# Issuing a kernel's first block in the order of planned times, with one planned store for each unit's left-over rows

## The chip, the cores and the metric

The kernel runs on one core of a Trainium2 chip. The core has five engines with a queue each: PE (TensorE, matrix products), DVE (VectorE), ACT (ScalarE), POOL (GpSimd) and SP (SyncE, which here only issues DMA transfers). Each queue is worked off in order. The metric is the device time of one execution in microseconds (us); lower is better.

## The reference

Eight batches of eight heads with 576 rows of 64 numbers each go through a linear attention, and its output through a feed-forward layer, all in 32-bit floats:

```python
q_s = softmax(q, over the 64 numbers of a row)
k_s = softmax(k, over the 576 rows)
kv = einsum('bhsd,bhse->bhde', k_s, v)            # 64 x 64 per head
x = einsum('bhsd,bhde->bhse', q_s, kv)            # as 4608 tokens x 512
h = x @ w_in                                      # 512 x 2048
r = maximum(h, 0.0)
out = (s * (r * r) + b) @ w_out                   # 2048 x 512
```

## The kernel before

A **unit** u is two heads of one batch; a **pair** is two units, so a batch is two pairs. A **block** is the first 512 rows of one batch; the 64 rows of each batch that are left over (the "left-over x") are gathered in the DRAM tensor `xleft` and become a ninth block at the end. The feed-forward layer of a block runs in 16 **steps** t, one for each 128 columns of `w_in`: the four groups `h` of a step (12 products, line 1006, into PSUM tile `h`), then ACT and DVE make `r`, `gh`, `gl` out of `h`, then the four groups `o` (12 products with `w_out`, line 1069, into PSUM tile `acc`). In what follows "step 4's h" means these 12 products.

The first block is special, because everything is still arriving. `fetch(f)` loads the 512 KB of `w_in` and the 512 KB of `w_out` of step f into a tile `st`; `conv_w(f)` splits them into a high and a low part with three operations on ACT (lines 238, 245, 253) and three on DVE (lines 242, 248, 255). `q_stream(u)` makes the x of unit u: softmax of q, a turn on PE (`qT`), a copy to SBUF (`early`, line 468), the product with kv (`xp`, line 475), then ACT writes the high part of x (line 481) and the left-over rows into a corner of the tile `misc` (line 273, in `keep_left`), and DVE the low part (line 484). `k_stream` and `kv_stream` do the keys of pairs 0 and 1, `k_pair` and `kv_second` those of pairs 2 and 3. Pairs 0 and 1 are batch 0, whose x the first block needs; pairs 2 and 3 are batch 1, for the second block. Pairs 2 and 3 are loaded (`reload`) over the SBUF area of pair 0, so each waits until the pair before has been used.

The order of all queues comes from a planner, the class `Order`: each of these functions is a stream of operations `Op(engine, planned cost, due, needs, ...)`, and the planner picks the next one. For the first 451 operations it picks nothing: `FIRST` is a written list of stream numbers, and the next operation of that stream is issued, whatever the times. Each engine's queue then holds its operations in the order of that list. The instructions that an operation issues on other engines than its own are not known to the plan: `q_stream`'s ACT operation calls `keep_left`, which, once both units of a pair are there, issues the store of the left-over x on SP (line 280); `load_v`, an SP operation, issues three memsets on POOL for pair 2 (lines 310 to 312); `q_stream`'s exponential issues a memset on POOL (line 451), and `k_exp` another (line 520).

While PE waits early on, the planner fills in products whose result nobody reads (`unused`, line 1196), until the first `h` takes their PSUM tile.

Of the kernel before, what the change touches and what calls it, by code (L numbers as in the profile page):

```python
# [25 lines left out]
def attention_moe(ctx: ExitStack, tc: tile.TileContext, q, k, v, w_in, w_out, s, b, out):  # L26
    nc = tc.nc
# [3 lines left out]
    P = 128  # L31
# [11 lines left out]
    DUE_R = (-150.0, -149.0, -148.0, -140.0, -139.0, -138.0, -50.0, -49.0, -48.0, 0.0, 1.0, 2.0)  # L43
    DUE_SB, DUE_L = -60.0, {"sb": -150.0}
    FIRST = (
# [12 lines left out]
    )  # L58
    ON_ACT = (-1.0, -1.0, 1.0, -1.0, -1.0, 1.0, 1.0, 1.0, -1.0, 1.0, -1.0, 1.0, -1.0, -1.0, -1.0, 1.0)
    PACE = 6  # L60
    KN_ON = ('ACT', 'ACT', 'ACT', 'ACT')
    QF_ON = ('ACT', 'DVE', 'ACT', 'ACT', 'DVE', 'ACT', 'DVE', 'DVE')
    WARM = 0
# [45 lines left out]
    def v_tile(t):  # L109
        m = 4 * NQ * (D + 1)  # L110
        return t[:, 0:m].rearrange("p (h n e) -> p h n e", h=4, n=NQ), t[:, m:VW].rearrange("p (h e) -> p h e", h=4)
# [156 lines left out]
    def keep_left(u, x):  # L268
# [6 lines left out]
        if len(there) == 2 and pr < NP:  # L275
            store_left(pr)

    def store_left(pr):
        bb, hq = divmod(pr, NP // 2)
        nc.sync.dma_start(xleft[:, 2 * hq:2 * hq + 2, bb * LEFT:(bb + 1) * LEFT], xl_.pop(pr)[0])  # L280
# [25 lines left out]
    def load_v(pr):  # L306
        main, left = sources(pr)
        vt, rest = v_tile(tiles[pr][2])
        if pr == NP // 2:
            nc.gpsimd.memset(rest[LEFT:P, :, 0:D], 0.0)  # L310
            nc.gpsimd.memset(vt[:, :, :, D:D + 1], 1.0)
            nc.gpsimd.memset(rest[:, :, D:D + 1], 1.0)
        for h in range(4):
            nc.sync.dma_start(vt[:, h, :, 0:D], main(v, h, 1)[:, 0])
        nc.sync.dma_start(rest[0:LEFT, :, 0:D], left(v, 0, 4))
# [119 lines left out]
    def q_stream(u):  # L435
# [38 lines left out]
        for a, src in enumerate((slice(0, HB), slice(HB, S))):  # L474
# [3 lines left out]
            )  # L478
        yield Op("ACT", 0.62, due)
        xh, xl = [t[:, hp, :].rearrange("p (a c) -> p a c", a=2) for t in (xh, xl)]  # L480
        nc.scalar.copy(xh, xp[:, :, 0:HB])
        keep_left(u, xp[:, 1, HB:HB + LEFT])
        yield Op("DVE", 0.6, due, free=[tag], gives=[f"x{u}"])
# [668 lines left out]
    def reload(pr):  # L1152

        p = 0 if pr == NP // 2 else pr - 1

        def v_():
            yield Op("SP", 3.2, DUE_R[3 * pr + 2], needs=[f"kv{p}"], gives=[f"v{pr} there"], dma=(0.62,) * 4 + (0.3,))
            load_v(pr)

        return whole(pr, 0, "k", DUE_R[3 * pr], [f"kv{p}"]), whole(pr, 1, "q", DUE_R[3 * pr + 1], [f"qe{2 * p}", f"qe{2 * p + 1}"]), v_()  # L1160
# [43 lines left out]
    with tc.manual_schedule(engines={E.PE, E.DVE, E.Activation, E.Pool, E.SP}):  # L1204
# [6 lines left out]
            + [k_stream(u) for u in range(NP)] + [k_pair(pr) for pr in range(NP // 2, NP)]  # L1211
            + [q_stream(u) for u in range(2 * NP)]
            + [kv_stream(pr) for pr in range(NP // 2)] + [kv_second(pr) for pr in range(NP // 2, NP)]
# [37 lines left out]
```

## Time and profile before

| | |
|---|---|
| median of 3 runs | 882.7 us (882.3 to 883.28) |
| profiled execution | 881.91 us, span of the trace 880.1 us |
| PE busy | 851.9 us (97%) |
| DVE busy | 600.3 us (68%) |
| ACT busy | 435.5 us (49%) |
| DMA, share of 16 engines in the main queue | 31.4% |

Times in the trace are counted from the start of the span. A timeline row gives start, length, engine, line, operation, tiles, the number of instructions merged in it, and in brackets how long the engine sat idle before it and who ended that. "SPq" is the issue of a DMA, not the transfer.

### The profile page before, as it was taken

The page shows a single profiled execution, that of the slowest core. Times are in us where ns is not written, and L with a number is a line of the kernel's source. Part 1 is how long each engine was busy: PE and PEld are TensorE (multiplying, and loading weights), DVE is VectorE, ACT ScalarE, POOL GpSimd, SP SyncE. Part 2 cuts the span into 40 slices and gives each one's busy share as a digit, 9 for nine tenths or more (in the row PEclk, how much of TensorE's full clock was granted, in tenths as well). Part 3 has the DMA queues.
Part 4 walks back from the last instruction along what each step waited for, and adds up shares of the span by engine and source line. Part 5 has one row for each costly group of instructions (what it writes and reads, how often), then busy time and mean ns, then how long its engine had stood idle before and what let it go on. Part 6 is the DMA issues. An engine that isn't in the chain of part 4 may idle for free.

```text
span 880.1 us, 11806 instructions
## 1 busy us (share of the span) xinstructions
PE 851.9 (97%) x4385; PEld 702.1 (80%) x4385; DVE 600.3 (68%) x920; ACT 435.5 (49%) x736; POOL 167.3 (19%) x185
## 2 busy tenths in 40 slices
PE   7779989999999999999999999999999999999997
PEld 6567868888888888888888888888888878888886
DVE  5767867677879676869576956696677686765400
ACT  4767966453645444544444544363445465555300
POOL 1000000211112020202011201111023436872000
PEclk9979999999999999999999999999999999999999
DMA  8559043433444523352244314342430110000100
GB/s 255 161 181 346 8 147 85 132 82 92 102 137 91 131 73 112 73 127 61 75 90 127 75 46 129 89 105 63 129 88 1 51 48 1 1 1 0 49 25 24
DMA packets 106572, 79.45 MB, mean 90 GB/s; under 512 B 56212, under 2 KB 100244, under 8 KB 106388
## 3 DMA queue, kind: packets, MB, share of 16 engines
q1 hardware_dynamic: 105360, 77.60, 31.4%
q10 hardware_dynamic: 1156, 1.11, 0.4%
q8 instruction: 34, 0.56, 0.3%
q14 instruction: 22, 0.18, 0.1%
HBM read 60.29 MB, written 18.40 MB: 89 GB/s over the span
## 4 chain that ended last, share of the span: by engine, by line
PE 87%; DMA 4%; ACT 3%; DVE 2%; issue 1%; SPq 1%; POOL 0%; ACTq 0%; POOLq 0%; DVEq 0%
PE acc L1069 37%; PE h L1006 33%; PE q L896 6%; PE last L992 5%; DMA st<-in_moe_w_out_dram 3%; PE kv L328 2%; PE qa L896 1%; DMA st<-in_moe_w_in_dram 1%; PE xp L711 1%; PE xq L711 1%; PE xp L475 1%; ACT st L245 0%; ACT low L238 0%; PE kT L363 0%; ACT w L253 0%
## 5 line engine op out<-in xcount | busy, mean ns | idle before, releaser
L1006 PE MATMUL h<-x,w 128*128 128x512 f32 x1344 | 331.8, 394 | 6.2 <-ACT r L1031 5.6
L1069 PE MATMUL acc<-w,gh 128*128 128x512 f32 x1024 | 318.4, 392 | 0.0
L1006 PEld LDWEIGHTS h<-x,w 128*128 128x128 f32 x1344 | 253.1, 190 | 60.8 <-ACT r L1031 6.8
L1069 PEld LDWEIGHTS acc<-w,gh 128*128 128x128 f32 x1024 | 190.9, 188 | 39.3
L1069 PE MATMUL acc<-w,gl 128*128 128x512 f32 x512 | 199.7, 390 | 0.0
L1031 ACT ACTIVATE r<-h 128x512 f32<-128x512 f32 x112 | 66.9, 597 | 190.8 <-PE h L1006 186.6
L1044 DVE SCALAR_TENSOR_TENSOR r<-r,sb 128x512 f32<-128x512 f32 x105 | 82.5, 786 | 91.9 <-ACT r L1031 91.1
L1069 PEld LDWEIGHTS acc<-w,gl 128*128 128x128 f32 x512 | 96.2, 188 | 20.3
L1048 DVE SCALAR_TENSOR_TENSOR gl<-r,sb,gh 128x512 fp32r<-128x512 f32 x105 | 84.9, 808 | 32.4 <-ACT gh L1046 31.4
L1046 ACT ACTIVATE gh<-r,sb 128x512 fp32r<-128x512 f32 x105 | 76.0, 724 | 53.2 <-DVE r L1044 51.0
L610 POOL TENSOR_TENSOR area<-area,qm 128x640 f32<-128x640 f32 x24 | 32.7, 1374 | 153.0 <-DVE qm L608 147.1
L627 POOL TENSOR_TENSOR qe<-qe,qr 128x640 f32<-128x640 f32 x24 | 32.8, 1366 | 63.3 <-DVE qr L623 34.3
L992 PE MATMUL last<-w 128*128 128x512 f32 x192 | 43.7, 389 | 0.0
L992 PEld LDWEIGHTS last<-w 128*128 128x128 f32 x192 | 36.0, 188 | 7.5
L691 POOL TENSOR_TENSOR spare<-kvf,spare 128x256 fp32r<-128x256 f32 x12 | 10.3, 860 | 134.3 <-issue 125.6
L238 ACT ACTIVATE low<-st 128x1024 int32<-128x1024 uint32 (+1 forms) x17 | 18.4, 1091 | 22.4 <-DMA st<-in_moe_w_out_dram 21.2
L328 PEld LDWEIGHTS kv<-area 128*64 128x64 f32 x600 | 20.1, 143 | 9.7 <-issue 8.4
L966 DVE SCALAR_TENSOR_TENSOR gl<-r,sb,gh 128x512 fp32r<-128x512 f32 x16 | 16.2, 1015 | 16.7 <-ACT gh L964 16.7
L717 ACT COPY y<-xp 64x320 f32<-64x320 f32 x48 | 20.2, 421 | 14.8 <-PE xp L711 14.3
L597 ACT ACTIVATE area<-area 128x640 f32<-128x640 f32 x24 | 17.7, 737 | 18.5 <-DVE area L559 18.5
L328 PE MATMUL kv<-area 128*64 128x65 f32 (+1 forms) x600 | 22.4, 230 | 4.5 <-DMA area<-in_v_dram 3.0
L721 DVE TENSOR_TENSOR y<-xp,y 64x320 f32<-64x320 f32 x48 | 23.4, 488 | 1.1
(185 smaller groups left out, 1046.0 us busy)
## 6 DMA issues: line engine op xcount, KB each, us to landing
st<-in_moe_w_in_dram SPq DMA_DIRECT2D x16, 512.0 KB, 7.6
st<-in_moe_w_out_dram SPq DMA_DIRECT2D x16, 512.0 KB, 7.3
out_dram<-o SPq DMA_DIRECT2D x16, 512.0 KB, 2.6
turned<-area SPq DMA_DIRECT2D x24, 320.0 KB, 2.3
qT<-turned SPq DMA_DIRECT2D x48, 160.0 KB, 3.2
area<-in_k_dram SPq DMA_DIRECT2D x14, 512.0 KB, 4.4
area<-in_q_dram SPq DMA_DIRECT2D x14, 512.0 KB, 5.6
area<-in_v_dram SPq DMA_DIRECT2D x56, 128.0 KB, 4.9
```

Source lines behind the costliest of these rows:

```text
L328: nc.tensor.matmul(kv[h * D:(h + 1) * D, i], kt[:, i, h, n], vt(2 * i + h, n), start=(n == 0), stop=(n == NT - 1))
L610: nc.gpsimd.tensor_tensor(out=qt, in0=qt, in1=bc(qm, [P, 2, NT, D]), op=ALU.subtract)
L627: nc.gpsimd.tensor_tensor(out=qe_, in0=qe_, in1=qr, op=ALU.mult)
L721: nc.vector.tensor_tensor(out=y[half[h], at], in0=parts[h][a][half[h]], in1=y[half[h], at], op=ALU.add)
L896: nc.tensor.matmul(BANK[where], w(a)[:, c * P:(c + 1) * P], xs[b_][:, c], start=k in (0, 1, 3) and n == 0, stop=n == 5, skip_group_check=True)
L992: nc.tensor.matmul(t_, g[:, js], w_, start=(f == 0 and i == 0), stop=(f == NFC - 1 and i == 2))
L1006: nc.tensor.matmul(hp_, w[:, j, c, :], x[:, c, :], start=(c == 0 and i == 0), stop=(c == NP - 1 and i == 2))
L1031: nc.scalar.activation(r, hp_, AF.Relu)
L1044: nc.vector.scalar_tensor_tensor(out=r, in0=r, scalar=s_col, in1=r, op0=ALU.mult, op1=ALU.mult)
L1046: nc.scalar.activation(gh, r, AF.Identity, bias=b_col)
L1048: nc.vector.scalar_tensor_tensor(out=gl, in0=r, scalar=b_col, in1=gh.bitcast(F32), op0=ALU.add, op1=ALU.subtract)
L1069: nc.tensor.matmul(acc[blk, j // 2][:, j % 2], g[:, js], w_, start=(f == 0 and i == 0), stop=(f == NFC - 1 and i == 2))
```

## The change

`FIRST` is written anew. It now has 452 entries, and operations of different streams alternate in it in the order of their planned times, where before the operations of one stream often stood in runs. The store of the left-over x becomes a stream of its own, `left_out(u)`, one for each of the units 0 to 7, with an SP operation that the list places like any other; the memsets of pair 2's v become a POOL operation of the stream that loads it. Four entries of two small tables flip: `QF_ON` says on which engine `qT` of a unit is copied (units 5 and 6 trade places), `ON_ACT` whether a step's square is made on ACT or DVE (steps 6 and 11 go to DVE, step 12 to ACT).

```diff
+    DUE_O = (0.0,) * 8
     FIRST = (
-        0, 54, 54, 18, 0, 55, 55, 0, 2, 1, 48, 48, 54, 54, 54, 54, 31, 48, 55, 55, 31, 55, 48, 48, 1, 31, 1, 19, 49, 49, 49, 31, 31, 23, 56, 62, 56, 55, 54, 54,
...
+        0, 18, 0, 2, 19, 0, 1, 54, 23, 54, 48, 54, 55, 21, 55, 48, 20, 54, 48, 54, 55, 3, 48, 54, 31, 22, 49, 55, 48, 31, 1, 3, 55, 54, 31, 49, 4, 56, 49, 6,
...
-    ON_ACT = (-1.0, -1.0, 1.0, -1.0, -1.0, 1.0, 1.0, 1.0, -1.0, 1.0, -1.0, 1.0, -1.0, -1.0, -1.0, 1.0)
+    ON_ACT = (-1.0, -1.0, 1.0, -1.0, -1.0, 1.0, -1.0, 1.0, -1.0, 1.0, -1.0, -1.0, 1.0, -1.0, -1.0, 1.0)
-    QF_ON = ('ACT', 'DVE', 'ACT', 'ACT', 'DVE', 'ACT', 'DVE', 'DVE')
+    QF_ON = ('ACT', 'DVE', 'ACT', 'ACT', 'DVE', 'DVE', 'ACT', 'DVE')
...
+    def left_of(u):
+        return bits[:, u % 4 * LEFT:(u % 4 + 1) * LEFT]
+
+    def left_out(u):
+        bb, hp = divmod(u, NP)
+        yield Op("SP", 0.65, DUE_O[u], needs=[f"left{u} there"], gives=[f"out{u}"], dma=(0.1,))
+        nc.sync.dma_start(xleft[:, hp, bb * LEFT:(bb + 1) * LEFT], left_of(u))
...
     def load_v(pr):
-        if pr == NP // 2:
-            nc.gpsimd.memset(rest[LEFT:P, :, 0:D], 0.0)
-            nc.gpsimd.memset(vt[:, :, :, D:D + 1], 1.0)
-            nc.gpsimd.memset(rest[:, :, D:D + 1], 1.0)
...
-        yield Op("ACT", 0.62, due)
+        yield Op("ACT", 0.82, due, needs=[f"out{u - 4}"] if u >= 4 else (), gives=[f"left{u} there"])
-        keep_left(u, xp[:, 1, HB:HB + LEFT])
+        nc.scalar.copy(left_of(u), xp[:, 1, HB:HB + LEFT])
...
         def v_():
+            if pr == NP // 2:
+                yield Op("POOL", 1.0, DUE_R[3 * pr + 2], needs=[f"kv{p}"])
+                vt, rest = v_tile(tiles[pr][2])
+                nc.gpsimd.memset(rest[LEFT:P, :, 0:D], 0.0)
+                nc.gpsimd.memset(vt[:, :, :, D:D + 1], 1.0)
+                nc.gpsimd.memset(rest[:, :, D:D + 1], 1.0)
...
-            + [q_stream(u) for u in range(2 * NP)]
+            + [q_stream(u) for u in range(2 * NP)] + [left_out(u) for u in range(2 * NP)]
```

On PE the order of the first block stays nearly what it was, and the number of products that are not fillers stays exactly the same; the fillers go from 59 to 47. On ACT and DVE neighbours change places. The queues that change much are SP and POOL.

SP's queue while x of batch 0 is made, before. `st_438`, `st_370`, `st_116` and `st_539` hold the weights of steps 4, 2, 0 and 3; q and v are pair 2's; `xleft<-misc` is the store of the left-over x (units 0 and 1 the first time, 2 and 3 the second).

```order
L280 DMA xleft<-misc 128x2x64
L222 DMA st_438<-in_moe_w_in_dram 128x4x256
L224 DMA st_438<-in_moe_w_out_dram 128x1024
L224 DMA st_370<-in_moe_w_out_dram 128x1024
L303 DMA area<-in_q_dram 128x4x256
L304 DMA area<-in_q_dram 64x4x64
L224 DMA st_116<-in_moe_w_out_dram 128x1024
L280 DMA xleft<-misc 128x2x64
L222 DMA st_539<-in_moe_w_in_dram 128x4x256
L224 DMA st_539<-in_moe_w_out_dram 128x1024
L314 DMA area<-in_v_dram 128x4x64 x4
L315 DMA area<-in_v_dram 64x4x64
```

The same place after the change; `st_230`, `st_225`, `st_108` and `st_377` are the weights of steps 4, 2, 0 and 3, and k is pair 2's.

```order
L225 DMA st_230<-in_moe_w_out_dram 128x1024
L312 DMA area<-in_k_dram 128x4x256
L313 DMA area<-in_k_dram 64x4x64
L225 DMA st_225<-in_moe_w_out_dram 128x1024
L312 DMA area<-in_q_dram 128x4x256
L313 DMA area<-in_q_dram 64x4x64
L225 DMA st_108<-in_moe_w_out_dram 128x1024
L223 DMA st_377<-in_moe_w_in_dram 128x4x256
L225 DMA st_377<-in_moe_w_out_dram 128x1024
L319 DMA area<-in_v_dram 128x4x64 x4
L320 DMA area<-in_v_dram 64x4x64
L285 DMA xleft<-misc 128x64
```

No store stands between k and v of pair 2 any more; the first one, unit 0's alone, comes behind v. Step 4's weights have moved in front of k (their first half stands further up, in front of pair 1's v).

SP's queue around the last weights of the first block, before. `st_1082`, `st_1084` and `st_1091` are steps 13, 14 and 15; v is pair 3's; the store is that of units 4 and 5.

```order
L314 DMA area<-in_v_dram 128x4x64 x4
L315 DMA area<-in_v_dram 64x4x64
L280 DMA xleft<-misc 128x2x64
L222 DMA st_1082<-in_moe_w_in_dram 128x4x256
L222 DMA st_1084<-in_moe_w_in_dram 128x4x256
L224 DMA st_1084<-in_moe_w_out_dram 128x1024
L224 DMA st_1082<-in_moe_w_out_dram 128x1024
L222 DMA st_1091<-in_moe_w_in_dram 128x4x256
L224 DMA st_1091<-in_moe_w_out_dram 128x1024
```

And after the change, where `st_927`, `st_922` and `st_1046` are steps 13, 14 and 15 and the store is unit 4's alone.

```order
L223 DMA st_922<-in_moe_w_in_dram 128x4x256
L223 DMA st_927<-in_moe_w_in_dram 128x4x256
L285 DMA xleft<-misc 128x64
L225 DMA st_922<-in_moe_w_out_dram 128x1024
L225 DMA st_927<-in_moe_w_out_dram 128x1024
L319 DMA area<-in_v_dram 128x4x64 x4
L320 DMA area<-in_v_dram 64x4x64
L223 DMA st_1046<-in_moe_w_in_dram 128x4x256
L225 DMA st_1046<-in_moe_w_out_dram 128x1024
```

Two of the six weight transfers have moved in front of the store, and v behind it. The copy on ACT for which the store waits has moved too: before, it stood in front of step 10's `r`, now it stands behind step 8's.

POOL's queue, before: the memsets of units 2 and 3 (`qe_244`, `qe_361`), those behind pair 2's exponentials of k (line 520), those of pair 2's v (lines 310 to 312), and unit 5's (`qe_611`).

```order
L451 MEMSET qe_244 128x10
L451 MEMSET qe_361 128x10
L520 MEMSET area 64x2x64 x2
L310 MEMSET area 64x4x64
L311 MEMSET area 128x16
L312 MEMSET area 128x4
L451 MEMSET qe_611 128x10
```

After the change, with lines 456, 525 and 1165 to 1167 in these roles:

```order
L456 MEMSET qe_270 128x10
L1165 MEMSET area 64x4x64
L1166 MEMSET area 128x16
L1167 MEMSET area 128x4
L456 MEMSET qe_360 128x10
L525 MEMSET area 64x2x64 x2
L456 MEMSET qe_597 128x10
```

The memsets for v have moved from behind pair 2's exponentials to in front of unit 3's memset.

## Rows read from the trace of the kernel before

**Rows 1.** The page: PE's busy time, share and instructions, and the 40 slices of 22 us, PE's busy tenths and the granted clock in tenths.

```profile
PE 851.9 (97%) x4385; PEld 702.1 (80%) x4385; DVE 600.3 (68%) x920; ACT 435.5 (49%) x736; POOL 167.3 (19%) x185
PE   7779989999999999999999999999999999999997
PEclk9979999999999999999999999999999999999999
```

**Rows 2.** What PE waited for from 0 to 130 us: total, times, longest.

```profile
PE h L1006 <- ACT r L1031: 5.6, 3, 3.7
PE xp L475 <- ACT early L468: 4.2, 2, 3.9
PE kv L328 <- DMA area<-in_v_dram: 3.0, 2, 2.1
```

**Rows 3.** PE's timeline from 28 to 153 us, the rows at which the stretches of the argument begin.

```profile
28.87 1.39 PE L328 MATMUL kv<-raw 128*64 128x64 f32 x40
...
38.49 1.24 PE L475 MATMUL xp<-early,kvf 128*128 128x256 f32 x4 [3.86 <-ACT early L468]
...
45.50 3.52 PE L1006 MATMUL h<-x,w 128*128 128x512 f32 x12 [0.26 <-ACT r L1031]
...
56.56 0.30 PE L328 MATMUL kv<-area 128*64 128x65 f32 x2 [2.10 <-DMA area<-in_v_dram]
...
68.24 0.62 PE L1069 MATMUL acc<-w,gh 128*128 128x512 f32 x2
...
72.80 3.01 PE L1006 MATMUL h<-x,w 128*128 128x512 f32 x12 [1.67 <-ACT r L1031]
...
79.24 2.88 PE L1006 MATMUL h<-x,w 128*128 128x512 f32 x12
81.96 0.62 PE L1069 MATMUL acc<-w,gh 128*128 128x512 f32 x2
...
124.29 4.60 PE L1006 MATMUL h<-x,w 128*128 128x512 f32 x12 [3.67 <-ACT r L1031]
...
132.03 2.88 PE L1006 MATMUL h<-x,w 128*128 128x512 f32 x12
...
152.48 2.88 PE L1006 MATMUL h<-x,w 128*128 128x512 f32 x12
```

**Rows 4.** What SP's queue waited for from 0 to 130 us: total, times, longest.

```profile
SPq L280 <- ACT misc L273: 39.5, 3, 24.4
...
SPq L314 <- POOL qe L451: 10.9, 1, 10.9
```

**Rows 5.** SP's timeline, the issues on either side of its long waits (a start and the time of issuing).

```profile
21.69 0.61 SPq L304 DMA_DIRECT2D area<-in_k_dram  x1
29.60 0.37 SPq L280 DMA_DIRECT2D xleft<-misc  x1
30.02 0.46 SPq L222 DMA_DIRECT2D st<-in_moe_w_in_dram  x1
...
42.47 0.50 SPq L224 DMA_DIRECT2D st<-in_moe_w_out_dram  x1
53.82 2.61 SPq L314 DMA_DIRECT2D area<-in_v_dram  x4
...
85.55 2.48 SPq L315 DMA_DIRECT2D area<-in_v_dram  x1
112.49 0.39 SPq L280 DMA_DIRECT2D xleft<-misc  x1
```

**Rows 6.** The chain that ended last, in order of time: its transfers of weights in this stretch (start, us from issue to landing).

```profile
32.90 7.23 DMA st<-in_moe_w_out_dram
...
60.14 9.87 DMA st<-in_moe_w_out_dram
...
114.31 6.21 DMA st<-in_moe_w_out_dram
```

**Rows 7.** ACT's timeline from the copy of unit 2's `qT` to step 0's `r`, the rows before which it sat idle, and the first.

```profile
31.46 0.64 ACT L468 COPY early<-qT 128x576 f32<-128x576 f32 x1
35.55 2.37 ACT L238 ACTIVATE low<-st 128x1024 int32<-128x1024 uint32 x2 [3.44 <-DMA st<-in_moe_w_out_dram]
...
40.21 0.71 ACT L238 ACTIVATE low<-st 128x512 int32<-128x512 uint32 x1 [1.17 <-DMA st<-in_moe_w_out_dram]
...
41.75 1.71 ACT L245 ACTIVATE st<-st 128x512 f32<-128x512 f32 x2 [0.24 <-DVE st L242]
44.85 0.60 ACT L1031 ACTIVATE r<-h 128x512 f32<-128x512 f32 x1 [1.39 <-PE h L1006]
```

**Rows 8.** DVE's timeline: step 2's `gl`.

```profile
59.28 0.68 DVE L1041 TENSOR_TENSOR gl<-r,gh 128x512 fp32r<-128x512 f32 x1
```

**Rows 9.** Stretches of 10 us: busy time (and instructions) of PE, PE's weight loads, DVE, ACT, POOL; granted clock; DMA share; GB/s.

```profile
20.00:30.00 10.00, 9.38 (x136) 7.72 (x134) 9.85 (x18) 8.81 (x21) 0.28 (x1) 1.00 0.43 122
...
60.00:70.00 10.00, 9.65 (x56) 8.14 (x57) 0.00 (x0) 0.00 (x0) 0.00 (x0) 0.82 1.04 370
70.00:80.00 10.00, 8.21 (x38) 6.26 (x38) 7.98 (x13) 9.87 (x15) 0.23 (x1) 1.00 1.08 350
80.00:90.00 10.00, 10.00 (x46) 8.17 (x45) 9.86 (x15) 9.15 (x14) 0.00 (x0) 1.00 1.00 277
90.00:100.00 10.00, 10.00 (x49) 8.22 (x49) 8.64 (x11) 9.83 (x13) 0.12 (x1) 1.00 0.00 0
```

22 rows, old and new, of the table FIRST are left out of this document.

## The prediction

> **What bounds the kernel now.** I read the page first: PE is busy for 97% of the span, and the slices in which it is not, and in which its clock is not full, are nearly all in the first six, 130 us [rows 1]. So the question is only what PE loses there, since the change leaves PE's products the same but for fillers. The list of PE's waits names three kinds: products `h` waiting for `r`, `xp` for the copy `early`, `kv` for the transfer of v [rows 2]. PE's timeline gives the places: a gap of 3.86 us before 38.49, then slow products; 2.10 us at 56.56 and more around it; 1.67 us at 72.80; 3.67 us at 124.29, after which 12 products take 4.60 us instead of 2.88 [rows 3]. From 132.03 to 152.48 and on there is no gap.
>
> None of these has its cause on PE, ACT or DVE. ACT and DVE did nothing at all from 60 to 70 us, while the DMA engines ran at 370 GB/s [rows 9]: the work waited for weights. And the weights were late because SP's queue stood still, as SP's own waits show: 39.5 us in three waits for the copy on ACT (line 273) whose result the store of the left-over x carries, and 10.9 us for POOL, which had to do pair 2's memsets first [rows 4]. SP's timeline gives the places: nothing issued from 22.30 (21.69 + 0.61) to 29.60, from 42.97 to 53.82, and from 88.03 to 112.49 [rows 5]. The chain shows what came of it: the last transfer of step 0's `w_out` was issued at 32.90 and landed at 40.13, another landed at 70.01, another at 120.52 [rows 6], and each landing is where ACT wakes.
>
> **The change, step by step.** The stores leave the places where they blocked, and the memsets for v come as soon as pair 0's kv is done. I follow the new order with the old durations, in four stretches, each from one row to the next.
>
> *To step 0's `r` (44.85 before).* On ACT, from the end of unit 2's copy, 32.10 (31.46 + 0.64), to `r` at 44.85 are 12.75 us, of which it sat idle 3.44 + 1.17 + 0.24 + 1.39 = 6.24 [rows 7]; 6.5 us is work, and the change keeps these operations. Ahead of it, pair 1's kv (28.87) now stands behind one of step 0's groups, a quarter of 2.72 us (81.96 − 79.24) [rows 3], so the start moves to 32.8. Without the waits `r` comes at 39.3, **5.6 us** earlier. Are the weights there? Before, from the restart at 30.02 to the landing at 40.13 took 10.1 us, with step 4's weights first [rows 5, 6]. Now SP goes on at 22.3, and step 4's weights are already in the queue: the landing is at about 32.4, and 2.8 us later (1.05 MB at 370 GB/s [rows 9]) if those still have to be worked off. ACT wants them about 3.4 us after 32.8, at 36.2. The wait on DMA goes either way.
>
> *To step 1's last group and step 2's first `o` (68.24 before, 23.4 us after `r`).* On ACT and DVE, from that `r` to the end of step 2's `gl` (59.28 + 0.68 = 59.96) took 15.1 us [rows 7, 8] without a long DMA wait; that stays. PE has in this time three times h, one `kv` of 1.39, two times four groups of o or h, in all 5 × 2.72 + 1.39 + 0.3 = 15.3. The two hand results to each other, so I take 15.7. What falls away is the wait for pair 2's v, issued at 53.82 before [rows 5]; now it follows step 3's weights and lands before 40, and PE wants it at about 48. Step 2's o starts at 39.3 + 15.7 = 55.0, and this stretch gives 23.4 − 15.7 = **7.7 us**.
>
> *To step 14's `h` (132.03 before, 63.8 us later).* PE has nine h and ten o, 19 × 2.72 = 51.7, and three turns of q, two `xp` and two turns of maxima, which take 0.2 to 1.0 each in the same timeline, 4.1 in all: 55.8. Before, the stretch held the waits of 1.67 and 3.67 and the slow products behind the latter. The weights of steps 5 to 8 now follow v at about 1.4 us each and land from about 39 to 48, wanted from 54 on. The long block of 24.4 us is replaced by a store whose copy on ACT stands behind step 8's `r`, about 85.5 by this count, with only two weights of steps 13 and 14 behind it; by the 6.21 us of the last chain transfer [rows 6] they land by 94, wanted at about 97, behind step 10's `r`. So no wait: **8.0 us**. ACT and DVE must keep up: from 70 to 100 us they were busy 9.6 and 8.8 of 10 on average while PE had no gap behind 72.80 [rows 3, 9]. They can, barely.
>
> *To the second block's first `h` (152.48 before).* PE's work is the same. But unit 6's `xp` now comes only three products (0.68 us) behind pair 3's kv, with about 0.3 us on DVE and 1.0 on ACT between them; before, twelve products stood there. I take a loss of **0.9 us**; none if ACT is early, 2 if it is busy.
>
> Nothing else counts. Eight stores instead of four cost SP 4 × 0.4 us [rows 5] that hides behind the transfers. The memsets now stand ahead of unit 3's on POOL and wait for pair 0's kv; unit 3's memset waited for unit 1's turn on PE anyway, which PE does behind pair 0's kv in both orders. The flipped table entries move some 1.4 us from ACT to DVE over three steps, hidden where PE leads. Beyond 152 us PE was without gaps, so the whole gain is kept.
>
> The sum: 5.6 + 7.7 + 8.0 − 0.9 = 20.4 us. The profiled execution took 881.9, 0.8 less than the median of 882.7; I take the sum off the median and forecast **862.4 us**.
>
> The best possible: from 28.87 to 132.03 are 103.2 us, and PE's full-rate work in it is 25 × 2.72 + 10.4 of small products = 78.4, so 24.7 us can go, 858. The forecast leaves 3.4 us of gaps in it.
>
> *A page weighed against a row.* The fillers end earlier, at step 0's first group, and gaps of up to about 1 us stay between short products from 30 to 40 us. From 20 to 30 us the clock was at its full 2.4 GHz with 136 short products, most of them turns, and 9.38 us busy [rows 9]; behind the gaps of 3.67 and 3.86 us it was not. The Trainium skill, "TensorE: Matmul & The Clock Gate", part 4, says transposes don't count as busy for the clock; by that the stretch after 30 us would be slow, and the sum 865.4 (priced below) instead of 862.4. The rows of 20 to 30 us speak against it. What it would do is a rival below.
>
> **Rivals.**
> - *ACT and DVE become the bound.* Before, they had paused 10 us ahead of the full stretch; now they run through from 30 us. ACT's 9.87 of 10 from 70 to 80 [rows 9] speaks for it, PE's gapless run beside it against. If each of ten steps loses 0.5 us: 867.4.
> - *The transfers are the bound.* Moving step 4's weights ahead delays k and q of pair 2. If the landing that I put at 32.4 takes twice its 10.1 us, `r` is back where it was at 5.6 us more: 868. Against it: the DMA share was 0.43 from 20 to 30 us [rows 9], so there is room.
> - *The clock stays low from 30 to 45 us.* Step 1's h would take 3.52 [rows 3] to twice 2.72: about 3 us, 865.4.
> - *The change does not do what it says*: SP is stuck elsewhere, for instance at the load of pair 3's q, which waits for unit 4's exponential and has all weights from step 9 on behind it, and gives half of the gain back: 872.
> - *Slower.* Pair 3's v has moved behind that store and lands at about 95 instead of 88. The second block hangs on it through kv and unit 6. It decides only from a landing after 118, where kv stands, and makes the kernel slower than before only after 139: 885. No row shows a transfer 40 us late except behind a blocked SP.
>
> **How the numbers follow.** Forecast 0.62 (859 to 866), ACT and DVE 0.13, transfers 0.10, clock 0.06, half given back 0.05, slower 0.04. The range of 858.5 to 870 leaves out the last two and the tail. A measurement of this kernel can tell about 0.2% from no change, 1.8 us. Faster by more: 0.94; within: 0.02; slower: 0.04.
>
> **What would show it.** Right: in SP's timeline no gap over 5 us before 40 us, and stores that wait for nothing that another transfer needs; ACT's idle time for weights under 3 us where it was about 20; step 0's `r` near 39, step 2's o near 55, step 14's h near 111, the second block's first h near 132; PE's granted clock full from 30 us on. A first `r` after 42, or ACT or DVE named as releaser of PE in many small waits, would prove the sum wrong in its first or third term; a long wait at unit 6's `xp` the fourth. What would upset it altogether is a new wait of SP on an engine, in front of weights.

## The result

| | before | changed |
|---|---|---|
| median, run together | 882.5 us (880.07 to 883.28, 4 runs) | 860.33 us (860.12 to 860.66, 4 runs) |
| profiled execution, its span | 881.91, 880.1 | 860.22, 858.4 |
| ratio | | 0.9754, 95% interval 0.9734 to 0.9773 |

The change makes the kernel 2.5% faster. The forecast was 862.4 us, with a range of 858.5 to 870.

The page of the changed kernel answers [rows 1]: PE's busy time, its 40 slices (here of 21.5 us), and the granted clock.

```profile
PE 843.3 (98%) x4373; PEld 695.9 (81%) x4373; DVE 601.3 (70%) x921; ACT 434.5 (51%) x734; POOL 171.1 (20%) x185
PE   7899999999999999999999999999999999999997
PEclk9999999999999999999999999999999999999999
```

PE is busy for 8.6 us less although its products are the same but for twelve fillers of about 0.1 us each: the slow ones are gone. ACT and DVE are as busy as they were. Of the first six slices, 7, 7, 7, 9, 9, 8 before, two below 9 are left, and no slice has a low clock.

What PE waited for from 0 to 130 us answers [rows 2] (total, times, longest; left out are two waits ahead of 13 us).

```profile
PE xp L480 <- ACT early L473: 1.4, 2, 1.1
PE h L1011 <- DVE x L489: 1.0, 1, 1.0
PE xp L480 <- ACT kvf L350: 0.5, 1, 0.5
PE kn L381 <- ACT qe L457: 0.5, 1, 0.5
PE h L1011 <- ACT r L1036: 0.5, 1, 0.5
```

No transfer stands in this list any more, and the waits for `r`, 5.6 us before, are 0.5. PE's timeline has the marks of the four stretches, as in [rows 3] (lines are 5 higher in the changed file):

```profile
38.55 3.02 PE L1011 MATMUL h<-x,w 128*128 128x512 f32 x12 [0.47 <-ACT r L1036]
...
53.84 0.62 PE L1074 MATMUL acc<-w,gh 128*128 128x512 f32 x2
...
109.78 2.88 PE L1011 MATMUL h<-x,w 128*128 128x512 f32 x12
...
117.35 1.39 PE L333 MATMUL kv<-area 128*64 128x65 f32 x40
118.66 0.97 PE L1011 MATMUL h<-x,w 128*128 128x512 f32 x3
120.12 1.24 PE L480 MATMUL xp<-early,kvf 128*128 128x256 f32 x4 [0.49 <-ACT kvf L350]
...
130.97 2.88 PE L1011 MATMUL h<-x,w 128*128 128x512 f32 x12
```

From 38.55, where the wait of 0.47 ends, to 119 us no row has a bracket: PE never waits. SP's timeline answers [rows 5], its waits from 0 to 130 us [rows 4]:

```profile
20.62 1.50 SPq L313 DMA_DIRECT2D area<-in_k_dram  x1
22.17 0.60 SPq L225 DMA_DIRECT2D st<-in_moe_w_out_dram  x1
...
25.70 0.34 SPq L225 DMA_DIRECT2D st<-in_moe_w_out_dram  x1
...
29.32 5.56 SPq L319 DMA_DIRECT2D area<-in_v_dram  x4
...
37.10 0.55 SPq L285 DMA_DIRECT2D xleft<-misc  x1
...
63.56 7.44 SPq L223 DMA_DIRECT2D st<-in_moe_w_in_dram  x2
86.15 0.34 SPq L285 DMA_DIRECT2D xleft<-misc  x1
86.54 0.90 SPq L225 DMA_DIRECT2D st<-in_moe_w_out_dram  x2
```

```profile
SPq L312 <- PE kv L333: 32.0, 3, 24.6
SPq L285 <- ACT misc L487: 15.1, 1, 15.1
```

SP still waits for a store, 15.1 us from 71.0 (63.56 + 7.44) to 86.15, and this costs nothing, since only the `w_out` of steps 13 and 14, pair 3's v and the last weight stand behind it. What changed is not that SP waits less, but what stands behind it when it does. Pair 2's v is issued at 29.32 instead of 53.82.

Stretches of 10 us, which answer [rows 9] (busy time of PE, its weight loads, DVE, ACT, POOL; granted clock; DMA share; GB/s):

```profile
20.00:30.00 10.00, 9.20 (x105) 7.31 (x101) 9.88 (x19) 9.53 (x24) 0.83 (x4) 1.00 1.08 323
30.00:40.00 10.00, 7.51 (x32) 5.15 (x33) 9.05 (x15) 8.27 (x15) 0.00 (x0) 1.00 1.01 253
40.00:50.00 10.00, 10.00 (x79) 8.14 (x79) 9.92 (x13) 9.97 (x14) 0.59 (x4) 1.00 1.05 363
50.00:60.00 10.00, 10.00 (x48) 8.31 (x47) 9.21 (x15) 8.07 (x10) 0.12 (x1) 1.00 0.83 270
60.00:70.00 10.00, 10.00 (x47) 8.18 (x46) 8.59 (x13) 9.61 (x15) 0.00 (x0) 1.00 0.99 318
70.00:80.00 10.00, 10.00 (x48) 8.29 (x47) 9.54 (x14) 9.02 (x13) 0.00 (x0) 1.00 0.37 113
```

Before, the transfers ran at 122 GB/s from 20 to 30 us and at 350 to 370 from 60 to 80; now they run at 253 to 363 GB/s all the way from 20 to 70. DVE and ACT, idle from 60 to 70 us before, are full from 40 to 50 us, and PE beside them has no gap.

### The profile page after: what moved, and what is told of

Its sections match the earlier page's. It is cut to its first block, busy times and chain, and to the rows that moved or that the text cites. A ratio compares the mean times of both kernels' runs of the same rounds, so it can differ in the third digit from the quotient of the medians.

```text
span 858.4 us, 11791 instructions
## 1 busy us (share of the span) xinstructions
PE 843.3 (98%) x4373; PEld 695.9 (81%) x4373; DVE 601.3 (70%) x921; ACT 434.5 (51%) x734; POOL 171.1 (20%) x185
## 3 DMA queue, kind: packets, MB, share of 16 engines
q10 hardware_dynamic: 1156, 1.11, 0.4%
## 4 chain that ended last, share of the span: by engine, by line
PE 93%; DMA 3%; DVE 1%; ACT 1%; issue 1%; SPq 1%; ACTq 0%; DVEq 0%
PE acc L1074 40%; PE h L1011 36%; PE q L901 7%; PE last L997 5%; PE kv L333 2%; DMA area<-in_q_dram 2%; DMA st<-in_moe_w_in_dram 1%; PE qa L901 1%; PE xp L716 1%; PE xq L716 1%; PE xp L480 0%; DVE w L971 0%; SPq L313 0%; PE qT L470 0%; DVE misc L960 0%
## 5 line engine op out<-in xcount | busy, mean ns | idle before, releaser
L1074 PEld LDWEIGHTS acc<-w,gl 128*128 128x128 f32 x512 | 96.2, 188 | 20.2
L604 POOL MEMSET area<- 64x128 f32 x24 | 4.8, 200 | 102.4 <-issue 74.8
L722 ACT COPY y<-xp 64x320 f32<-64x320 f32 x48 | 20.2, 420 | 9.6 <-PE xp L716 8.9
L734 DVE TENSOR_TENSOR x<-y,x 128x512 fp32r<-128x512 f32 x24 | 23.4, 975 | 0.0
L1100 ACT COPY last<-last 128x512 f32<-128x512 f32 x3 | 1.8, 587 | 42.7 <-PE last L997 42.7
```

The source lines that it names most:

```text
L734: nc.vector.tensor_tensor(out=xl, in0=x, in1=xh.bitcast(F32), op=ALU.subtract)
L1074: nc.tensor.matmul(acc[blk, j // 2][:, j % 2], g[:, js], w_, start=(f == 0 and i == 0), stop=(f == NFC - 1 and i == 2))
```

## The experiments

For each kernel, the table gives the median and range of its runs, and from its profile step 0's `r` and the three stretches behind it: to step 2's first `o`, on to step 14's first `h`, on to the second block's first `h`. From there to the end of the span it was 727.2 to 727.7 us in every profile, so the four columns hold all of the difference but for some tenths.

| kernel | us | `r` | to `o` of 2 | to `h` of 14 | to `h` of 16 | span |
|---|---|---|---|---|---|---|
| before | 882.5 | 44.85 | 23.39 | 63.79 | 20.45 | 880.1 |
| changed | 860.33 | 37.90 | 15.94 | 55.94 | 21.19 | 858.4 |
| before again | 879.05 | 44.15 | 23.43 | 61.58 | 20.45 | 877.3 |
| stores alone | 869.27 (868.62 to 870.93) | 38.23 | 23.39 | 57.68 | 20.45 | 867.4 |
| memset alone | 872.51 (871.49 to 873.01) | 44.84 | 15.94 | 62.20 | 20.45 | 871.1 |
| stores and memset | 860.97 (860.13 to 862.13) | 38.75 | 15.95 | 56.01 | 20.45 | 858.8 |
| order alone | 860.23 (859.48 to 860.81) | 38.67 | 15.95 | 55.94 | 21.20 | 859.0 |
| stores early | 862.25 (860.31 to 863.19) | 39.85 | 16.97 | 55.94 | 21.20 | 861.4 |
| tables old | 860.32 (860.12 to 861.58) | 37.72 | 15.94 | 56.14 | 21.48 | 858.7 |
| memset in v | 859.76 (859.29 to 860.73) | 37.89 | 15.94 | 55.94 | 21.20 | 858.3 |
| less ahead | 860.47 (859.73 to 861.18) | 36.98 | 16.17 | 55.94 | 21.20 | 857.9 |
| xp later | 861.88 (861.41 to 862.56) | 37.70 | 15.93 | 55.94 | 23.12 | 860.1 |
| changed again | 860.63 (860.18 to 862.28) | 40.01 | 15.93 | 55.94 | 21.20 | 860.5 |
| kv behind h | 861.07 (860.79 to 863.21) | 38.12 | 15.93 | 55.94 | 21.92 | 859.3 |

Times are counted from each span's start; beside them the kernel before ran at medians of 880.9 to 882.1 us, 878.1 to 885.3 in single runs.

**Stores alone.** Each unit's store becomes a stream of its own in the kernel before; all else stays.

```diff
-        keep_left(u, xp[:, 1, HB:HB + LEFT])
+        nc.scalar.copy(left_of(u), xp[:, 1, HB:HB + LEFT])
...
-        9, 9, 7, 7, 37, 39, 37, 59,
+        9, 9, 7, 7, 383, 384, 385, 386, 37, 39, 37, 59,
...
-        61, 45, 45, 17, 47, 47, 60, 80,
+        61, 45, 45, 17, 387, 388, 47, 47, 60, 80,
```

> The kernel before, with each unit's store as an operation of its own (those of units 0 to 3 issued behind weight 5's w_out, those of 4 and 5 behind weight 15's); the order of all other operations, the memset and the tables stay. Theory of the prediction: SP is no longer held from 22.30 to 29.60 nor from 33.5 to 41.54, so step 0's r comes at 39 to 40 instead of 44.85 (5 to 6 us), pair 2's v still waits for the memset until about 48, and some of the third stretch goes too (W13 and W14 land earlier): 868 to 873 us. Rival (the gain comes from the new order of the operations on PE, ACT and DVE): 880 to 883 us, and r within 1 us of 44.85.

Measured 869.27 us, ratio 0.9866 (0.9846 to 0.9887): as the theory says, in its places too. `r` comes at 38.23, the second stretch keeps its 23.39, the third gives 6.1 of the 63.79. The first row is SP's timeline, the second PE's, the third SP's list of waits:

```profile
47.35 2.60 SPq L322 DMA_DIRECT2D area<-in_v_dram  x4
```

```profile
50.24 0.30 PE L336 MATMUL kv<-area 128*64 128x65 f32 x2 [2.89 <-ACT w L253]
```

```profile
SPq L322 <- POOL qe L459: 19.6, 1, 19.6
```

What SP was held by before is gone, and it runs into the next wait the sooner: pair 2's v now waits 19.6 us for POOL instead of 10.9.

**Memset alone.** In the kernel before, the memset becomes an operation of POOL's own, placed behind pair 0's kv.

```diff
+                yield Op("POOL", 1.0, DUE_R[3 * pr + 2], needs=[f"kv{p}"])
...
-        50, 50, 20, 62, 62, 50, 50, 56,
+        50, 50, 20, 62, 27, 62, 50, 50, 56,
```

> The kernel before, with only the memset as an operation of POOL's own right behind pair 0's kv; stores, order and tables stay. Theory of the prediction: step 0's r stays at 44.8 (within 0.5 us), since the stores hold SP as before; pair 2's v is issued at about 43 instead of 53.82, and the stretch from r to step 2's first o shrinks from 23.4 to 15 to 17 us; the third stretch loses little: 871 to 876 us. Rival 1 (v2 was not what PE waited for in this stretch): 881 to 883 us. Rival 2 (the loads behind v2, now 10 us earlier, free the third stretch as well): 865 to 869 us.

Measured 872.51 us, ratio 0.9899 (0.9880 to 0.9918). `r` stays at 44.84, and the second stretch is 15.94 us, the changed kernel's to the hundredth. SP's timeline, then PE's:

```profile
43.91 2.79 SPq L310 DMA_DIRECT2D area<-in_v_dram  x4
```

```profile
115.23 4.61 PE L1002 MATMUL h<-x,w 128*128 128x512 f32 x12 [3.45 <-ACT r L1027]
```

The store of units 4 and 5 still holds what stands behind it, and PE's wait for it and the slow products behind it are still there: the third stretch gives only 1.6 us, less than the 2.2 by which the two profiles of the kernel before differ in it.

**Stores and memset.** Both edits in the kernel before; its order of everything else and its tables stay.

> The kernel before with both: each unit's store as an operation of its own, and the memset ahead of pair 2's v; the old order of all other operations and the old two tables of engines stay. Theory of the prediction (the queue of SP is what the 20 us were lost in): 861 to 864 us, within 0.5% of the changed kernel's 860.3, with the first 29 us as in the kernel before. Rival (the new order of PE, ACT and DVE earns a good part of the gain): 867 us or more.

Measured 860.97 us, ratio 0.9772 (0.9752 to 0.9791). Alone, against the 881.1 us run beside them, the parts gave 11.9 and 8.6 us, in sum 20.5; together 20.2. The new order of PE, ACT and DVE isn't needed for any of it that a measurement can tell.

**Order alone.** The reverse: the new list and tables, with the store and the memset where the code of before has them (a pair's store at its second unit's copy, the memset inside the load of v). The list is the changed kernel's without the entries of the new operations.

> The kernel before with only the changed kernel's order and its two tables: a store still belongs to the copy of the second unit of a pair and is issued there, and the memset still belongs to the load of pair 2's v. In the new order the store of units 0 and 1 comes behind pair 2's v (before, it came ahead of weight 2), that of units 4 and 5 ahead of the w_out of weights 14 and 13 alone. Theory (what cost 20 us was what stood behind the waiting issues in SP's queue, and the order alone changes that): 859.5 to 861.5 us, as the kernel with the new operations alone, 860.97. Rival (the stores need to be operations of their own, since a pair's store waits for its later unit): 865 us or more.

Measured 860.23 us, ratio 0.9751 (0.9728 to 0.9775). SP's timeline:

```profile
29.49 5.53 SPq L314 DMA_DIRECT2D area<-in_v_dram  x4
...
37.24 1.06 SPq L280 DMA_DIRECT2D xleft<-misc  x2
...
86.93 0.37 SPq L280 DMA_DIRECT2D xleft<-misc  x1
```

So neither half of the change is needed if the other is there. The stores had only to leave the places in front of the weights, and the memset its place on POOL; new operations placed well do it, and so does a list in which the old ones stand later or earlier.

**Stores early.** The changed kernel with the stores of units 0 and 1 back behind pair 2's k.

```diff
-        56, 4, 33, 54, 26, 51, 57, 51, 55, 33, 54, 2, 55, 57, 54, 51, 5, 33, 71, 55, 57, 5, 51, 33, 74, 27, 55, 71, 57,
+        56, 33, 54, 51, 57, 51, 55, 33, 54, 55, 57, 54, 51, 33, 71, 55, 57, 51, 33, 74, 55, 62, 63, 4, 26, 2, 5, 5, 27, 71, 57,
```

> The changed kernel, with the stores of units 0 and 1 put back to where the kernel before has one, right behind pair 2's k in SP's order, so that everything behind them (weight 2's w_out, pair 2's q, weight 0's w_out, weight 3, pair 2's v) waits for unit 1's left-over copy, at 27.7 us in the changed kernel's trace, instead of starting at about 22. Theory: weight 0's w_out is issued at 29 to 31 us instead of 25.70, lands at 38 to 40 instead of 34.4, and step 0's r comes 2.5 to 5 us later than 37.90; the total 862.5 to 865.5 us. Rival (there is slack and the stall is hidden): within 0.5 us of 860.3.

Measured 862.25 us, ratio 0.9788 (0.9755 to 0.9820); `r` at 39.85, 1.95 us later, where 2.5 to 5 were expected, and the total just below what was expected. Its single runs, 860.31 to 863.19, reach down to the changed kernel's, so the loss is read from the places in the trace more than from the total. Its rows, of SP, ACT and PE:

```profile
25.61 3.45 SPq L285 DMA_DIRECT2D xleft<-misc  x2
...
30.74 0.59 SPq L225 DMA_DIRECT2D st<-in_moe_w_out_dram  x1
```

```profile
36.92 0.67 ACT L239 ACTIVATE low<-st 128x512 int32<-128x512 uint32 x1 [1.80 <-DMA st<-in_moe_w_out_dram]
```

```profile
37.92 1.89 PE L1011 MATMUL h<-x,w 128*128 128x512 f32 x5 [1.65 <-DVE x L489]
40.50 4.06 PE L1011 MATMUL h<-x,w 128*128 128x512 f32 x12 [0.26 <-ACT r L1036]
```

The wait has the place that the theory gives it: the issue of step 0's `w_out` is 5.0 us later than in the changed kernel, and ACT waits 1.80 us for its landing instead of 0.40. But 5 us late is not 5 us lost: ACT wakes 2.4 us later (36.92 for 34.48). The landing followed the issue by 6.2 us at most (30.74 to 36.92) instead of 8.8 (25.70 to 34.48). From 20 to 30 us the DMA share was 0.69 instead of 1.08; that less was in flight ahead of it would explain this, but was not tested. A further 1.0 us is lost in the second stretch, in products at a lower clock.

**Tables old.** The changed kernel with ON_ACT and QF_ON of before.

```diff
-    QF_ON = ('ACT', 'DVE', 'ACT', 'ACT', 'DVE', 'DVE', 'ACT', 'DVE')
+    QF_ON = ('ACT', 'DVE', 'ACT', 'ACT', 'DVE', 'ACT', 'DVE', 'DVE')
```

> The changed kernel with the two small tables as before (which engine copies the transposed q of units 5 and 6, and which of steps 6, 11 and 12 square on ScalarE); all else as changed. Theory: those choices lie on engines with room and move nothing: 860.3 us within 0.6. Rival (ScalarE or VectorE is at its limit between 70 and 117 us, and the choice was a part of the gain): 861.5 us or more.

Measured 860.32 us: no difference. In the profile the last two stretches are 0.2 and 0.3 us longer, less than a measurement can tell.

**Memset in v.** The changed kernel with the memset in `load_v` again; one 27 leaves the list.

> The changed kernel with the memset back inside the load of pair 2's v, at the place of that load in the program's order; all else as changed. Theory: pair 2's v waits for POOL again; in the changed order its load stands 2 to 3 us behind pair 1's kv's operands, so it is issued at 35 us or later instead of 29.3, and the loads of weights 5 and 7 behind it go with it: 863 to 870 us. Rival (the memset stood in the way only because of its old place in the order): within 0.6 us of 860.3.

Measured 859.76 us: here the theory was wrong and its rival right. POOL's timeline of this kernel shows why, and then that of the kernel before:

```profile
25.02 0.28 POOL L460 MEMSET qe<- 128x10 f32 x1 [7.98 <-ACT early L380]
25.36 0.31 POOL L319 MEMSET area<- 64x256 f32 x1
```

```profile
51.58 0.20 POOL L520 MEMSET area<- 64x128 f32 x1 [25.51 <-ACT area L519]
53.15 0.20 POOL L520 MEMSET area<- 64x128 f32 x1 [1.38 <-ACT area L519]
53.30 0.31 POOL L310 MEMSET area<- 64x256 f32 x1
```

In the new order the load stands in the list ahead of pair 2's exponentials, so on POOL its memset follows unit 3's at once. Before, it stood behind the two memsets of line 520, which wait for ACT to finish with pair 2's k. Those held it, not the work of the memset (53.30 to 53.83, 0.5 us) and not that it lay inside the load.

**Less ahead.** The changed kernel with four conversions later, off ACT and DVE in front of step 0's `r`.

```diff
-        71, 57, 33, 55, 57, 56, 71, 52, 56, 33, 36, 56, 52, 34, 57, 36, 62, 74,
+        71, 57, 55, 57, 56, 71, 52, 56, 33, 56, 52, 33, 34, 57, 62, 74,
...
-        75, 7, 34, 74, 75, 9, 52, 35,
+        75, 7, 34, 74, 36, 36, 75, 9, 52, 35,
```

> The changed kernel with four conversions on ScalarE and VectorE later: weight 1's last two behind unit 2's copy of the transposed q, and weight 4's first two behind step 0's gl (its product wants it first at 56.6 us). Theory: PE's gaps of 1.09, 0.29, 0.96 and 0.47 us between 30 and 39 us, which end with ACT's copy, unit 3's x and step 0's r, shrink by 1 to 2 us in sum, and nothing behind 39 us wants the moved ones earlier: 858.3 to 859.5 us. Rival 1: the gaps move on to weight 1's late conversion or to step 2's, 860 to 861. Rival 2: the opening is bound by the landing of weight 0's w_out, 34.4 us, and stays: 860 to 860.6.

Measured 860.47 us: no gain. PE's gap ahead of unit 2's `xp` is still 1.10 us, and ACT idles where the conversion was (ACT's timeline):

```profile
28.36 1.04 ACT L350 ACTIVATE kvf<-kv,z 64x64 f32<-64x64 f32 x4 [1.32 <-PE kv L333]
```

The conversion's time turned into idle time, so the gap is the way from PE's kv over ACT's two copies (kvf, then unit 2's `early`) back to PE, not ACT's load.

**xp later** and **kv behind h.** Two tries to win back the fourth stretch, in which the kernel before was 0.74 us quicker. The list is written out for the whole program, so that nothing else moves; the first moves unit 6's xp (stream 60) behind two more groups of h, the second pair 3's kv (73) behind step 13's last group (87) and unit 6's xp behind three groups of step 15's h (89).

```diff
-        60, 87, 188, 89, 60, 89, 87, 60, 89,
+        89, 89, 60, 60, 87, 188, 87, 60, 89,
```

```diff
-        65, 67, 73, 47, 61, 87, 186, 73, 61, 73, 61, 187, 87, 61, 60, 87, 188, 89, 60, 89, 87, 60, 89, 87, 61, 89,
+        65, 67, 87, 73, 47, 61, 87, 186, 87, 73, 61, 73, 61, 187, 61, 89, 89, 89, 87, 60, 188, 60, 87, 60, 89, 61,
```

> The changed kernel with unit 6's xp two more products (1.36 us) behind pair 3's kv on PE, and its two copies as much later; all else, the later blocks' order too, is held to the changed kernel's. Theory of the prediction's fourth step (the loss lies in the short way from pair 3's kv over DVE and ACT to unit 6's xp): PE's gap of 0.49 us at 120.12 goes, step 16's first h comes 0.4 to 0.5 us earlier than the 21.2 us behind step 14's first h, 20.7 to 20.8: about 859.8 us. Rival (ACT waits for the later xp and hands step 13's gh over later): the gap moves on and 21.2 us or more stay: 860.3 to 861.

> The changed kernel with pair 3's kv three products later on PE, behind all of step 13's h, and ScalarE's r of step 13 ahead of the pair's kvf, unit 6's xp behind nine products of step 15's h, and its copies behind step 13's gh; all else is held to the changed kernel's order. The run with xp alone moved showed PE waiting 1.31 us for r of step 13, which stood behind kvf on ScalarE, and 0.91 us for unit 6's x. Theory (the fourth stretch loses its 0.74 us because kvf stands ahead of r on ScalarE and xp follows kv too closely): both gaps go, step 14's h to step 16's h takes 20.45 us as in the kernel before instead of 21.19, and the total is 859.5 to 860.0. Rival (the wait only moves to unit 7's xp or to the next block): 21 us or more, 860.3 or more.

Measured 861.88 and 861.07 us: both rivals were right that the gap only moves; the first try is slower even than the 860.3 to 861 of its rival. The changed kernel had 860.33 and 860.63; the first try is slower by over 1 us, the second by less than its own spread, but neither is faster. PE's timeline of the first, then of the second:

```profile
120.73 1.65 PE L1011 MATMUL h<-x,w 128*128 128x512 f32 x6 [1.31 <-ACT r L1036]
...
124.96 0.74 PE L470 MATMUL qT<-ident,qe 128*128 128x128 f32 x5 [0.91 <-DVE x L489]
```

```profile
124.48 0.74 PE L470 MATMUL qT<-ident,qe 128*128 128x128 f32 x5 [0.91 <-DVE x L489]
```

In the changed kernel xp stood where PE would otherwise have waited for `r` of step 13, which follows kvf on ACT. Moved away, it leaves that wait open and makes unit 7's turn wait for unit 6's x. With kv later, the first wait is gone and the second stays. The stretch of 20.45 us that stores and memset keep comes with the whole old order there; that wasn't tried in the changed kernel.

**Before again** and **changed again**, for the first 20 us.

> The kernel before, unchanged, profiled once more. The changed kernel gained 1.1 to 1.4 us more than the prediction's sum, and its trace shows this ahead of 29 us: pair 0's kv starts at 18.78 instead of 19.91, and 10 to 15 us lie at a granted clock of 1.00 instead of 0.75. Theory (the opening's clock varies from run to run): in this second trace of the old order the stretch 10 to 15 us lies at another clock than 0.75, and pair 0's kv starts more than 0.5 us away from 19.91. Rival (the reordered opening earns it): again about 0.75, kv within 0.2 us of 19.91, and the span within 0.5 us of 880.1.

> The changed kernel, unchanged, timed and profiled beside the two others. Theory (the full clock at 10 to 15 us belonged to the one execution shown, and step 0's r does not hang on it): pair 0's kv at 19.4 to 19.8 instead of 18.78, but r again at 37.7 to 37.9 and the total within 0.5 us of 860.3. Rival (the new order makes the opening's clock): kv again near 18.8 with a clock of 1.00 at 10 to 15 us.

Measured 879.05 and 860.63 us. The stretches from 10 to 20 us of the changed kernel, in the first profile and in this one:

```profile
10.00:15.00 5.00, 2.26 (x28) 1.88 (x29) 4.90 (x10) 2.83 (x7) 0.00 (x0) 1.00 0.81 228
15.00:20.00 5.00, 4.93 (x79) 4.17 (x79) 4.96 (x10) 4.51 (x10) 0.12 (x1) 1.00 1.02 330
```

```profile
10.00:15.00 5.00, 1.71 (x9) 1.33 (x11) 4.88 (x8) 2.38 (x5) 0.00 (x0) 0.73 0.71 196
15.00:20.00 5.00, 5.00 (x39) 4.59 (x35) 3.42 (x7) 3.00 (x7) 0.12 (x1) 0.58 1.04 326
```

The same program has its opening at full clock in one execution and far below in another, and pair 0's kv starts at 18.78 and 21.75. So the full clock doesn't come with the order; whether the order makes it likelier stays open. But I had also expected `r` to stay at 37.7 to 37.9, and it came at 40.01: of the 2.97 us by which kv is late, 2.11 reach `r`, and this profiled execution, at 862.28, is the slowest of its kernel. For the kernel before, neither the theory nor its rival came out: kv starts at 19.47, 0.44 us from 19.91, at nearly the same clock (0.74 and 0.75), but the span is 2.8 us shorter. Of the 2.8 us between its two spans, 2.2 lie in the third stretch, where the 12 products behind the gap took 4.60 us in one execution and 3.03 in the other. The second execution's row on PE:

```profile
122.98 3.03 PE L1006 MATMUL h<-x,w 128*128 128x512 f32 x12 [3.22 <-ACT r L1031]
```

## Why the prediction was right, step by step

**What bounds the kernel** was right: PE, held up by SP's queue. Stores alone, memset alone and both show it without any other move. One of SP's standstills, from 33.50 to 41.54 for the second store, is missing from the prediction's list of places, though its 39.5 us include it.

**To `r`, 5.6 us predicted, 6.95 measured.** The waits were sized right. Counted from pair 0's kv, `r` came 24.9 us later before, 24.6 in memset alone, 19.0 and 19.1 with the stores moved: 5.5 to 6.0. Mis-sized was what came beside it. I put the start of the stretch 0.7 us later, since one of step 0's groups now stands ahead of pair 1's kv; but kv of pair 1 came 8.81 us behind that of pair 0 instead of 8.96, for the group took the place of fillers and idle time. That is 0.85 us. And the profiled execution had its opening at full clock, 1.1 us earlier at pair 0's kv, which I had left as it was; of this only 0.3 reached `r`, as the next paragraph shows. The last 0.2 to 0.3 us lie behind pair 1's kv.

**The landing of step 0's `w_out`**, put at 32.4 or 2.8 us later, was at 34.4 by the row in which ACT wakes; but ACT wanted it at 34.1, not at 36.2:

```profile
34.48 0.68 ACT L239 ACTIVATE low<-st 128x512 int32<-128x512 uint32 x1 [0.40 <-DMA st<-in_moe_w_out_dram]
```

Where the opening is early, ACT waits for it (0.20, 0.40 and 0.73 us in the three profiles with kv ahead of 19 us) and `r` follows kv by 18.9 to 19.5 us; where it is late, there is no wait and `r` follows by 18.3 (five profiles; stores early aside). So an opening that is 1.1 us earlier wins 0.3 at `r`. I had this wait hidden with 1 to 4 us to spare; there is none, and it came out small for a reason that the prediction doesn't have, since ACT and the transfer happen to be ready within some tenths of each other.

**To step 2's `o`, 7.7 predicted, 7.45 measured** (15.94 us for 15.7). Memset alone gives exactly this.

**To step 14's `h`, 8.0 predicted, 7.85 measured** (55.94 for 55.8). Stores alone give 6.1 of it. That it came so near is in part luck: the second profile of the kernel before took 61.58 us for this stretch where the first took 63.79, and against the second the gain is 5.6. SP's wait at unit 4's store ends at 86.15, where the prediction had 85.5, and nothing waits for what stands behind.

**To the second block, a loss of 0.9 predicted, 0.74 measured**, in every kernel with the new order and in none with the old one. The mechanism was told too narrowly: with xp later the loss grows, for `r` of step 13 waits behind kvf as well.

**The sum.** Predicted 20.4, on the marks 6.95 + 7.45 + 7.85 − 0.74 = 21.5, between the spans 21.7. The forecast was 2.07 us too high: 1.3 from the sum, most of it step 0's group; 0.8 because I took the sum off the median, not off the profiled execution, which was 0.8 lower; and 0.1 from a slip, since 882.7 − 20.4 is 862.3. (Less 0.1, as the changed kernel's median lies above its profiled run.) The gaps left up to step 14's h were put at 3.4 us; they are 1.09 + 0.29 + 0.96 + 0.47 = 2.8, from 30 to 39 us, and the 0.49 at 120.12 lies behind it. Between the two spans of the kernel before lie 2.8 us, so no agreement closer than that should be read into the sum.

**The rivals.** ACT and DVE are not the bound: 9.97 and 9.92 of 10 us busy from 40 to 50 beside a PE without a gap. The transfers ran at a DMA share above 1 from 20 to 50 us and cost ACT a wait of 0.40. SP does stand still, at a place where it costs nothing. Pair 3's v was no wait. The clock stayed at 1.00 from 30 us on, so the rival built on the Trainium skill, "TensorE: Matmul & The Clock Gate", part 4 (a transpose doesn't count as busy in the same way) fell here; the stretch from 15 to 20 us above, 79 products, about half of them turns and fillers, the others of kv, also lies at 1.00. The prediction's reading for this rival was wrong in one point: of the 136 products from 20 to 30 us before not most were turns, but 48, fillers included, and some 80 were of kv. So no stretch of turns alone was seen, and the runs don't settle what that sentence says. What the runs do show is a low clock behind idle time: in stores early, behind 1.65 us idle ahead of 37.92, the next 12 products took 4.06 us, and the granted clock from 40 to 50 us was 0.86; in the changed kernel, behind 0.96 us idle ahead of 36.20, they took 3.02 at 1.00.

**What the prediction didn't see** is that the new operations aren't needed: order alone and memset in v give the full gain without them. What counts is the place of each entry in its queue.

## What to carry to other kernels

When an engine idles for a transfer, look at when the transfer was issued and what stood ahead of it in the issuing queue; a small store that waits for a late result holds every 512 KB weight behind it. It isn't the waiting that costs, it's what is queued behind it: order such a queue by when each entry can go, and put the waiting entry in front of nothing that is wanted soon. The same holds for a small memset: its cost is the wait of the one ahead of it on its engine.

## What the runs showed of the hardware

The granted clock of the first 20 us differs from execution to execution of the same program: from 10 to 15 us it was 1.00 in three of the nine profiles with the new order and 0.71 to 0.82 in the other six, 0.74 to 0.92 in the five with the old. The start of pair 0's kv goes from 18.11 to 21.75 us, earliest in the three at 1.00; whether the order has a part in it stays open, as above.

Twelve equal products behind one and the same gap of the kernel before took 4.60 us in one execution and 3.03 in another, at a granted clock of 0.63 and 1.00, with the gap at 3.67 and 3.22 us. In the changed kernel the gap and the slow products behind it are gone, and its single runs lie closer together: 860.12 to 862.28 us (fewer runs) where those of before went from 878.06 to 885.28. That the gap made most of that spread is likely, but not shown.

Four issues of pair 2's v took SP 2.61 us before, at a DMA share of 0.30 in that time, and 5.56 in the changed kernel, at 1.08: 3 us longer, hidden here. With the stores alone, at 0.32, the same load took 2.60 us again. A high share alone doesn't explain it: the same four issues for pair 3's v took 2.60 us at 87.48 in the changed kernel, at a share of 0.90, and for a later pair 3.55 us at 121.16, at 1.11.
